# Routing of one batch and softmax of another in one timetable of joined runs, in an attention and mixture-of-experts kernel

## The chip, the cores and the metric

The kernel runs on one core of a Trainium2 chip, as a single launch. The time is the device time of one execution in microseconds (us); the median of several executions counts. TensorE (PE) does the matmuls and the transposes, with the weight loads (PEld) beside it; VectorE (DVE) and ScalarE (ACT) do the elementwise work; GpSimd (POOL) issues the indirect DMAs and SyncE (SP) the others.

## The reference

Three stages, all in float32. First a two-way attention without projections: 8 batches, 8 heads, 512 tokens `x` and 32 state rows per head, 64 wide. The tokens read the state (first softmax) and the state reads the tokens (second softmax). Then a feed-forward layer with hard-swish, 512 to 2048 to 512, over all 4608 rows. Then a mixture of 8 experts, one per row, with a second gate.

```python
scores = scale * np.matmul(x, state.transpose(0, 1, 3, 2))      # softmax -> a
xread = np.matmul(a, state)
scores2 = scale * np.matmul(state, x.transpose(0, 1, 3, 2))     # softmax -> a2
sread = np.matmul(a2, x)
...
h = x @ w_in
g = h * np.clip(h + 3.0, 0.0, 6.0) / 6.0
x = g @ w_out
...
logits = x @ w_gate
e_idx = np.argmax(logits, axis=1)
...
h = np.maximum(x[mask] @ w1[e], 0.0)
out[mask] = gate_w[mask, None] * eom[mask, e, None] * (h @ w2[e])
```

## The kernel before, in words

The work of the attention and the feed-forward layer is cut into segments, one per batch (`segs`, in the main loop at the end of what is printed below); batch 0 is cut in two halves of 8 f tiles, with batch 1 between them, and a last segment, of the rows that the states read, stands apart. An f tile is a slice of 128 of the 2048 hidden columns. For each f tile, `h_xread` makes six matmuls of 512 columns, `act` applies the hard-swish on ScalarE and VectorE (r at L419, g at L420, gh at L421, gl at L422), and `second` makes twelve matmuls in `gemm2` for the f tile two steps earlier, into four banks (o). These 18 matmuls of 512 columns are called the large ones here. `make_sw` multiplies the state into `w_in` once per four f tiles and batch: a run of eight small matmuls of shape 64\*32 (tile `misc`, operand `win`, L193), the state-weight run, whose result ScalarE (sh, L377) and VectorE (sl, L378) take out of two banks.

Into the segment of one batch are put two other pieces of work. The first is the routing of the batch before (`route`): the rows of its result are evicted (xr), turned by four transposes a tile of 128 rows (L460), copied (x2T, L461), multiplied with the two gates (the logits, L467, shape 128\*32), turned back (L473), and the expert is chosen by small steps of VectorE; two matmuls of 32 columns (L504, L505, the counts) give each row its place in its expert's list; then SP writes the rows (xd) and POOL scatters their token numbers into the table `tab` (L535). The second is the softmax of the next batch (`attn`): `attn_rows` begins with an x run (L193 with operand `xT`), scores of the state with the tokens, into two banks; VectorE transposes both (L273), finds the maxima of the second softmax (L317), ScalarE takes its exponentials (L321), and the first softmax follows in steps of 1024 elements (L287, L290, L291, L294, L299, L303, L307). `attn_cols` then turns the second softmax (L338), reads the tokens with it (L346, shape 128\*32, operand `xq`), and turns the result into x1 (L353), for heads e = 0 and 1 one after the other.

The bank `misc` has two buffers, which all small runs share; a list `users` holds who still reads the last ones. `halves`, used by the x run and the state-weight run, takes both buffers and makes its first matmul wait until both are free and all operands are there, so that the run isn't broken. All other small runs take one bank and are put where the framework's scheduler finds place. Both pieces of work are generators; the main loop takes one step of the routing from f tile 2 on and one of the softmax from f tile 3 on, one each per f tile (`step(later)`, `step(att)`). Each engine works its own queue in order.

Of the kernel before, what the change touches and what calls it, by code (L numbers as in the profile page):

```python
# [8 lines left out]
F32 = mybir.dt.float32  # L9
# [71 lines left out]
def tile_kernel(  # L81
# [60 lines left out]
    marks = []  # L142
# [13 lines left out]
    st_t, aT, loads, e2_t, x_in = {}, {}, {}, {}, {}  # L156

    def st_load(b):
        st_t[b] = ap.tile([128, 4, NS], F32, tag="st", name=f"st{b}")
        D.dma_start(st_t[b], sts[b])  # L160

    def x_loads(b):
        if b not in st_t:
            st_load(b)
        for k in range(2):
# [3 lines left out]
            loads[b, k] = x_t  # L169

    def q_loads(b):
        for k in range(2):
            x_q = ap.tile([128, 4, 256], F32, tag="x4", bufs=4, name=f"xq{b}_{k}")
            D.dma_start(x_q, xq[b, :, :, 256 * k:256 * k + 256])
# [7 lines left out]

    def halves(b, rhs, behind=()):

        behind = [*behind, *(i for u in users[-2:] for i in u)]
        made = [misc() for _ in range(2)]
        ps = [m[0] for m in made]
        first = None
        for j in range(4):
            for e in range(2):  # L190
                o = slice(64 * e, 64 * e + 64)
                r = rhs(j)[o]
                i = T.matmul(ps[e][32 * j:32 * j + 32, :r.shape[1]], st_t[b][o, j, :], r, start=True, stop=True,  # L193
                             tile_position=(64 * e, 32 * j))
                if first is not None:
                    tc.add_manual_dep(i.ins, first.name, LATER, reason="all at once")
                    continue
                first = i.ins
                for d in behind:
                    tc.add_manual_dep(first, d.name, DEP, reason="both banks are free and all of x is there")  # L200
        return ps, [m[1] for m in made]
# [109 lines left out]
    def columns(b, src, done=None):  # L311
# [3 lines left out]
        e2_t[b] = e2, s2, r2  # L315
        for e in range(2):
# [4 lines left out]
            j = S.activation(e2[e], src[e], AF.Exp, bias=nm[:, e:e + 1], scale=0.125, accum_out=s2[:, e:e + 1])  # L321
            if done:
                done[e] += [i.ins, j.ins]

    def attn_cols(b):
# [4 lines left out]
        e2, s2, r2 = e2_t.pop(b)  # L330
        x_q = [loads.pop((b, k, "q")) for k in range(2)]
        V.tensor_scalar(s2, s2, 1e-9, None, op0=ALU.add)
        V.reciprocal(r2, s2)
        read = ap.tile([128, 2, HD], F32, tag="wy", name="read", bufs=2)
        for e in range(2):
            psT, done = misc()
            for i in range(4):
# [816 lines left out]
```

## Time and profile before

| | us |
|---|---|
| median of 3 runs | 1150.56 |
| lowest and highest | 1149.32, 1151.2 |
| the profiled execution | 1145.18 |
| its span, first to last instruction | 1143.3 |
| TensorE busy | 1109.3 |
| VectorE busy | 697.5 |
| ScalarE busy | 559.9 |
| GpSimd busy | 137.0 |

The profile is of one execution. Busy time is the sum of an engine's instructions, with overlaps counted once. Matmuls are pipelined: each is shown with its full duration while the next one has begun, so that the distance of two starts is what a matmul costs. A run of equal instructions is one row with its count; a float32 matmul that TensorE makes in several passes is counted once a pass, so that a run of 16 read matmuls is shown as x32.

### The profile page before, as it was taken

What the parts mean: (1) busy time and instruction counts of PE and PEld (TensorE: products, weight loads), DVE (VectorE), ACT (ScalarE), POOL (GpSimd) and SP (SyncE); (2) the same over time, 40 slices, a digit from 0 to 9 for tenths busy, and PEclk for the clock granted to TensorE, in tenths of its full rate; (3) what the DMA queues carried; (4) which work ended last, traced back from release to release, by engine and by line L of the source; (5) the groups of instructions that cost most, each with busy time, mean ns of one, the idle gap of its engine ahead of it and who ended that gap; (6) DMA issues with size and microseconds to landing.
All of it is one profiled execution on the core that took longest, in us unless ns stands there. A gap on an engine that the chain in (4) does not pass through costs nothing.

```text
span 1143.3 us, 18670 instructions
## 1 busy us (share of the span) xinstructions
PE 1109.3 (97%) x7008; PEld 869.7 (76%) x7008; DVE 697.5 (61%) x1463; ACT 559.9 (49%) x1068; POOL 137.0 (12%) x172
## 2 busy tenths in 40 slices
PE   3899999999999999999999999999999999999997
PEld 1557776677677777777777788899969986999994
DVE  6997758744835736647445376876536644666661
ACT  3769734433333434433433345566546654666651
POOL 0000001010010100100101013242222212222101
PEclk9999999999999999999999999999999999999999
DMA  8834014210210211110101018386175768822400
GB/s 270 305 105 158 3 60 95 71 58 20 74 40 3 74 39 37 41 38 1 38 1 37 1 38 252 118 301 252 47 236 201 251 217 309 324 94 83 148 19 30
DMA packets 54463, 128.32 MB, mean 112 GB/s; under 512 B 6736, under 2 KB 25424, under 8 KB 54352
## 3 DMA queue, kind: packets, MB, share of 16 engines
q1 hardware_dynamic: 47072, 108.66, 28.7%
q0 software_dynamic: 7296, 18.41, 4.6%
q8 instruction: 57, 0.93, 0.4%
q14 instruction: 38, 0.31, 0.1%
HBM read 136.98 MB, written 19.57 MB: 137 GB/s over the span
## 4 chain that ended last, share of the span: by engine, by line
PE 89%; DVE 6%; ACT 1%; issue 1%; DMA 1%; SPq 0%; POOL 0%; POOLq 0%; ACTq 0%; DVEq 0%
PE h L797 16%; PE h L390 15%; PE o L429 10%; PE o L430 10%; PE o L428 10%; PE o L813 5%; PE o L817 5%; PE o L816 5%; PE misc L193 3%; PE h L404 2%; PE h L764 1%; PE misc L460 1%; PE misc L748 1%; PE o L783 1%; PE misc L346 1%
## 5 line engine op out<-in xcount | busy, mean ns | idle before, releaser
L429 PE MATMUL o<-wo,gh 128*128 128x512 f32 x512 | 203.6, 398 | 0.4 <-DVE wo L581 0.4
L428 PE MATMUL o<-wo,gh 128*128 128x512 f32 x512 | 199.8, 395 | 1.7 <-ACT wo L580 1.7
L430 PE MATMUL o<-wo,gl 128*128 128x512 f32 x512 | 200.5, 392 | 0.0
L420 DVE SCALAR_TENSOR_TENSOR g<-r,h 128x512 f32<-128x512 f32 x128 | 87.6, 684 | 116.1 <-ACT r L419 116.0
L803 DVE TENSOR_TENSOR vl<-w2s,vh 128x512 fp32r<-128x512 f32 x128 | 88.6, 692 | 106.2 <-ACT vh L802 87.3
L419 ACT ACTIVATE r<-h 128x512 f32<-128x512 f32 x128 | 76.5, 598 | 134.6 <-PE h L390 133.3
L802 ACT CAST vh<-w2s 128x512 fp32r<-128x512 f32 x128 | 79.4, 620 | 101.2 <-PE o L817 100.3
L422 DVE TENSOR_TENSOR gl<-g,gh 128x512 fp32r<-128x512 f32 x128 | 88.3, 690 | 53.7 <-ACT gh L421 53.0
L429 PEld LDWEIGHTS o<-wo,gh 128*128 128x128 f32 x512 | 96.2, 188 | 29.3 <-issue 9.4
L428 PEld LDWEIGHTS o<-wo,gh 128*128 128x128 f32 x512 | 95.8, 188 | 28.0 <-issue 4.4
L535 POOL DMA_INDIRECT tab<-toku,ldsti x34 | 34.4, 1011 | 658.9 <-DVE ldsti L530 593.8
L390 PE MATMUL h<-ah,sh 128*128 128x512 f32 x256 | 108.7, 426 | 4.5 <-ACT ah L256 3.0
L421 ACT CAST gh<-g 128x512 fp32r<-128x512 f32 x128 | 79.4, 620 | 68.1 <-DVE g L420 66.6
L430 PEld LDWEIGHTS o<-wo,gl 128*128 128x128 f32 x512 | 96.2, 188 | 20.2 <-issue 1.0
L793 DVE TENSOR_TENSOR wl<-w1s,wh 128x512 fp32r<-128x512 f32 x128 | 88.7, 693 | 30.0 <-ACT wh L792 23.3
L390 PE MATMUL h<-al,sh 128*128 128x512 f32 x256 | 102.9, 402 | 0.0
L390 PE MATMUL h<-ah,sl 128*128 128x512 f32 x256 | 100.8, 395 | 0.0
L817 PE MATMUL o<-vh,hl 128*128 128x512 f32 x256 | 100.3, 392 | 0.0
L816 PE MATMUL o<-vl,hh 128*128 128x512 f32 x256 | 100.1, 391 | 0.0
L792 ACT CAST wh<-w1s 128x512 fp32r<-128x512 f32 x128 | 79.5, 622 | 36.8 <-PE h L797 33.6
L797 PEld LDWEIGHTS h<-xh,wh 128*128 128x128 f32 x512 | 76.5, 188 | 11.7 <-issue 1.6
L797 PE MATMUL h<-xh,wh 128*128 128x256 f32 x512 | 82.8, 283 | 1.3 <-ACT xh L753 1.3
(223 smaller groups left out, 1829.8 us busy)
## 6 DMA issues: line engine op xcount, KB each, us to landing
w1s<-w SPq DMA_DIRECT2D x88, 512.0 KB
w2s<-w SPq DMA_DIRECT2D x88, 512.0 KB
xd<-xr SPq DMA_DIRECT2D x34, 256.5 KB
xT<-xT SPq DMA_DIRECT2D x16, 512.0 KB
wi<-w_in SPq DMA_DIRECT2D x16, 512.0 KB
wraw<-w_out SPq DMA_DIRECT2D x16, 512.0 KB
xq<-xq SPq DMA_DIRECT2D x16, 512.0 KB
half<-xp SPq DMA_DIRECT2D x4, 256.0 KB
```

The costliest lines, as they stand in the source:

```text
L390: T.matmul(ps, w[:, o:o + 128], a[:, e, :], start=(n == 0), stop=(n == 5))
L420: V.scalar_tensor_tensor(g6, r, 6.0, ps, op0=ALU.min, op1=ALU.mult)
L422: V.tensor_tensor(gl, g6, gh.bitcast(F32), op=ALU.subtract)
L428: T.matmul(po[t], gh[:, s], woh[ft], start=first, stop=False)
L429: T.matmul(po[t], gh[:, s], wol[ft], start=False, stop=False)
L430: T.matmul(po[t], gl[:, s], woh[ft], start=False, stop=last)
L792: S.copy(wh, a)
L793: V.tensor_tensor(wl, a, wh.bitcast(F32), op=ALU.subtract)
L797: T.matmul(ps, w[:, k, :], x[:, k, :], start=(m == 0), stop=(m == 11))
L803: V.tensor_tensor(vl, c, vh.bitcast(F32), op=ALU.subtract)
L816: T.matmul(py[t], hh[:, sl], vl, start=False, stop=False)
L817: T.matmul(py[t], hl[:, sl], vh, start=False, stop=(ft == 7))
```

## The change

The routing is cut into functions (`turn_rows`, `logits`, `turn_logits`, `choose`, `ranks`, `place`, `scatter`), and so is the second softmax (`cols_turn`, `cols_read`, `cols_x1`). `one_run` takes one or more such parts, allocates their banks, and issues all their matmuls behind each other; the first of them waits for the banks and the operands of all. In the segments of batches 2 to 6 a `timetable` says in which f tile each part is issued: at 2 and 3 the four transposed tiles of rows in two runs of eight; at 4 the x run; at 6 the turn of the columns for both e; at 7 the reads of both e and the logits of all four tiles as one run; at 8 x1 and the turn of the logits as one; the choice at 9, the counts at 10, rows and scatter at 11. In batch 7's segment there is no softmax, and the rest is done the same way. The second half of batch 0 has a table of its own. Batch 1's scatter moves from that half into batch 2's segment, behind the Relu of its fifth f tile, and that segment's x loads go behind an earlier Relu. The turned rows of tiles 2 and 3 take a buffer of the tag x4, which the loads of xT and xq share. No arithmetic is changed, and the matmuls are the same ones.

```diff
+    def x_loads(b, behind=()):
+        i = st_load(b)
+        for d in behind:
+            tc.add_manual_dep(i, d.name, DEP, reason="rows are written first")
...
+    def one_run(*parts):
+
+        behind = [i for u in users[-2:] for i in u]
+        built = [p() for p in parts]
+        first = None
+        for mms, needs, _ in built:
+            behind += needs
+        for mms, _, _ in built:
+            for m in mms:
+                i = m().ins
+                if first is not None:
+                    tc.add_manual_dep(i, first.name, LATER, reason="all at once")
+                    continue
+                first = i
+                for d in behind:
+                    tc.add_manual_dep(first, d.name, DEP, reason="banks are free and all operands are there")
+        for b in built:
+            b[2]()
+
+    def at_will(*parts):
+
+        for p in parts:
+            mms, _, use = p()
+            for m in mms:
+                m()
+            use()
...
+    def cols_turn(b):
+
+        e2, s2, r2, exps = e2_t.pop(b)
+        V.tensor_scalar(s2, s2, 1e-9, None, op0=ALU.add)
+        V.reciprocal(r2, s2)
+
+        def part():
...
+            return [lambda e=e, i=i: T.transpose(made[e][0][:, 128 * i:128 * i + 128],
+                                                 e2[e][:, 128 * i:128 * i + 128], ident)
+                    for e in range(2) for i in range(4)], exps, use
...
+            return [lambda e=e, i=i, j=j: mm(e, i, j) for e in range(2) for i in range(4) for j in range(4)], \
+                [*copies, *q_in[b]], use
...
-        read = ap.tile([128, 2, HD], F32, tag="wy", name="read", bufs=2)
-        for e in range(2):
-            psT, done = misc()
-            for i in range(4):
-                T.transpose(psT[:, 128 * i:128 * i + 128], e2[e][:, 128 * i:128 * i + 128], ident)
-            a2T = ap.tile([128, 4, 128], F32, tag="wy", name="a2T", bufs=2)
-            done.append(S.copy(a2T.rearrange("p a n -> p (a n)"), psT).ins)
-            yield
...
-            psR, done = misc()
-            for i in range(4):
-                for j in range(4):
-                    h = 2 * j + e
-                    T.matmul(psR[32 * j:32 * j + 32, :HD], a2T[:, i, 32 * j:32 * j + 32],
-                             x_q[h // 4][:, i, HD * (h % 4):HD * (h % 4) + HD], start=(i == 0), stop=(i == 3),
-                             tile_position=(0, 32 * j))
-            done.append(S.activation(read[:, e, :], psR[:, :HD], AF.Copy, scale=r2[:, e:e + 1]).ins)
-            yield
...
+        one_run(cols_turn(b))
+        yield
+        one_run(cols_read(b))
+        yield
+        one_run(cols_x1(b))
...
-        for t0 in range(0, nt, 2):
-            x2T = mp.tile([128, 4, 256], F32, tag="x2T", name="x2T", bufs=1)
-            for t in range(2):
-                ps, done = misc()
-                for k in range(4):
-                    T.transpose(ps[:, 128 * k:128 * k + 128], rows[t0 + t][:, 128 * k:128 * k + 128], ident)
-                done.append(V.tensor_copy(x2T[:, :, 128 * t:128 * t + 128],
-                                          ps.rearrange("p (k t) -> p k t", k=4)).ins)
-                if t == 0:
-                    yield
...
+            return [lambda t=t, k=k, ps=ps: T.transpose(ps[:, 128 * k:128 * k + 128],
+                                                        r.rows[t][:, 128 * k:128 * k + 128], ident)
+                    for t, (ps, _) in zip(ts, made) for k in range(4)], [r.made[t] for t in ts], use
...
+            return [lambda k=k, i=i: mm(k, i) for i in range(n // 2) for k in range(4)], list(r.copies), use
...
+    def scatter(r, behind=()):
 
         new = []
-        for t in range(nt):
-            i = G.indirect_dma_start(flat, bass.IndirectOffsetOnAxis(ap=dsti[:, t:t + 1], axis=0),
-                                     toku[:, tile0 + t:tile0 + t + 1], None).ins
+        for t in range(r.nt):
+            i = G.indirect_dma_start(flat, bass.IndirectOffsetOnAxis(ap=r.dsti[:, t:t + 1], axis=0),
+                                     toku[:, r.tile0 + t:r.tile0 + t + 1], None).ins
+            for d in behind:
+                tc.add_manual_dep(i, d.name, DEP, reason="rows are written first")
...
-        (1, 2): [I(10), go(cols[0], 2)],
-        (1, 3): [I(11), go(cols[0], 2)],
+        (1, 2): [I(10), go(cols[0])],
+        (1, 3): [I(11), go(cols[0])],
...
+    def timetable(b, r, att):
+
+        rows = attn_rows(b) if att else iter(())
+        todo = {}
+
+        def at(k, *fs):
+            todo.setdefault(k, []).extend(fs)
+
+        at(2, lambda: one_run(turn_rows(r, [0, 1])))
+        at(3, lambda: one_run(turn_rows(r, [2, 3], ap)))
+        for k in range(4, 10):
+            at(k, lambda: next(rows, None))
+        if att:
+            at(6, lambda: one_run(cols_turn(b)))
+            at(7, lambda: one_run(cols_read(b), logits(r, 0, 4)))
+            at(8, lambda: one_run(cols_x1(b), turn_logits(r, 0, 4)))
+        else:
+            at(6, lambda: one_run(logits(r, 0, 4)))
+            at(7, lambda: one_run(turn_logits(r, 0, 4)))
+        at(9, lambda: choose(r))
+        at(10, lambda: ranks(r))
+        at(11, lambda: place(r), lambda: scatter(r))
+        return todo
+
+    def half_timetable(b, r):
+
+        rows = attn_rows(b)
+        row = lambda: next(rows, None)
+        return {
+            2: [lambda: one_run(turn_rows(r, [0, 1]))],
+            3: [lambda: at_will(logits(r, 0, 2), turn_logits(r, 0, 2)), row],
+            4: [lambda: one_run(turn_rows(r, [2, 3])), row],
+            5: [lambda: at_will(logits(r, 2, 2), turn_logits(r, 2, 2)), lambda: choose(r), row],
+            6: [lambda: ranks(r), lambda: place(r), lambda: one_run(cols_turn(b)), row],
+            7: [lambda: one_run(cols_read(b)), row, row, lambda: one_run(cols_x1(b))],
+        }
...
-        att = [attn(nxt[0])] if n >= 2 and nxt[0] < NB else []
+        more = n >= 2 and nxt[0] < NB
+        late = n > 2
+        todo = {}
         for ft in range(f0, f1):
             h = h_xread(b, ft)
             with soon(b):
@@ -959,23 +1126,24 @@
             second(LAG)
             for x in plan.get((b, ft), []):
                 x()
-            if att and ft == f0 + 1:
-                x_loads(nxt[0])
-            if att and ft == f0 + 2:
+            if more and ft == f0 + 1 + late:
+                x_loads(nxt[0], marks[-2:-1] if n == 3 else ())
+            if n >= 2 and ft == f0 + 2:
+                r = later.pop()
+                todo = timetable(nxt[0], r, more) if late else half_timetable(nxt[0], r)
+                if n == 2:
+                    unplaced = r
+            if n == 3 and ft == f0 + 4:
+                scatter(unplaced, marks[-1:])
+            for x in todo.pop(ft - f0, []):
+                x()
+            if more and ft == f0 + 2 + late:
...
-            if ft - f0 >= 2:
-                step(later)
-            if ft - f0 >= 3:
-                step(att)
...
-        while att:
-            step(att)
-        while later:
-            step(later)
-        if nxt[0] < NB and n >= 2:
+        if more:
```

On TensorE, in batch 4's segment before, a logits run stands alone (its operand x2T holds two turned tiles of rows, l is its copied result), between large matmuls into h and o:

```order
L467 MATMUL misc<-x2T,wg_sb 32x256 x4
L390 MATMUL h<-al_3093,sh_1_1_3477 128x512
L390 MATMUL h<-ah_3092,sl_1_1_3478 128x512
L428 MATMUL o_3508<-wo_356,gh 128x512
L473 MATMUL misc<-ident,l_3573 128x128 x2
L429 MATMUL o_3508<-wo_356,gh 128x512
L430 MATMUL o_3508<-wo_356,gl 128x512
L428 MATMUL o_3509<-wo_356,gh 128x512
```

In the same segment after, the end of both reads (xq, with the turned second softmax a2T) and the logits of all four tiles:

```order
L386 MATMUL misc<-xq_0_3557,a2T 32x64 x2
L386 MATMUL misc<-xq_1_3559,a2T 32x64 x2
L553 MATMUL misc<-x2T,wg_sb 32x256 x8
L455 MATMUL h<-ah_3093,sh_2_0_3638 128x512
L455 MATMUL h<-al_3094,sh_2_0_3638 128x512
L455 MATMUL h<-ah_3093,sl_2_0_3639 128x512
```

The two logits runs and the two read runs have become one, ahead of a tile of h.

On VectorE, in batch 4's segment before, from the transposes behind the x run on (sm holds maxima and sums, bt the first softmax, x2T the turned rows):

```order
L273 STREAM_TRANSPOSE bt<-misc 128x512 x2
L317 TENSOR_REDUCE sm<-misc 128x1 x2
L320 TENSOR_SCALAR sm<-sm 128x1
L287 TENSOR_REDUCE sm<-bt 128x32
L320 TENSOR_SCALAR sm<-sm 128x1
L290 TENSOR_TENSOR bt<-bt,sm 128x1024
L461 COPY x2T<-misc 128x4x128
L420 SCALAR_TENSOR_TENSOR g_3644<-r,h 128x512
L294 TENSOR_REDUCE sm<-bt 128x32
L422 TENSOR_TENSOR gl<-g_3644,gh 128x512
L461 COPY x2T<-misc 128x4x128
```

The same place after:

```order
L301 STREAM_TRANSPOSE bt<-misc 128x512 x2
L345 TENSOR_REDUCE sm<-misc 128x1 x2
L348 TENSOR_SCALAR sm<-sm 128x1
L485 SCALAR_TENSOR_TENSOR g_3618<-r,h 128x512
L348 TENSOR_SCALAR sm<-sm 128x1
L315 TENSOR_REDUCE sm<-bt 128x32
L487 TENSOR_TENSOR gl<-g_3618,gh 128x512
L318 TENSOR_TENSOR bt<-bt,sm 128x1024
L357 TENSOR_SCALAR sm<-sm 128x2
L358 RECIPROCAL sm<-sm 128x2
L322 TENSOR_REDUCE sm<-bt 128x32
L443 TENSOR_TENSOR sl_2_0_3639<-misc,sh_2_0_3638 128x512
```

The copies of turned rows are gone from here, the whole chain of the first softmax up to its sum (L322) stands in one piece with one g and one gl in it, and right behind it come the subtractions sl of a state-weight run.

## Rows read from the trace of the kernel before

**Rows 1.** The page, busy us of an engine, share of the span and its instructions

```profile
PE 1109.3 (97%) x7008; PEld 869.7 (76%) x7008; DVE 697.5 (61%) x1463; ACT 559.9 (49%) x1068; POOL 137.0 (12%) x172
```

**Rows 2.** Stretch of one whole batch: busy us (instructions) by engine, granted clock, DMA

```profile
439.72:518.86 79.14, 78.88 (x481) 58.21 (x480) 44.96 (x95) 30.91 (x56) 3.82 (x4) 1.00 0.13 41
```

**Rows 3.** Timeline of TensorE, four transposes: start us, us, line, output<-operands, shape, count

```profile
518.86 0.60 PE L460 MATMUL misc<-ident,xr 128*128 128x128 f32 x4
519.21 0.48 PE L390 MATMUL h<-ah,sh 128*128 128x512 f32 x1
519.53 0.39 PE L390 MATMUL h<-al,sh 128*128 128x512 f32 x1
519.76 0.40 PE L390 MATMUL h<-ah,sl 128*128 128x512 f32 x1
```

**Rows 4.** The same view, eight transposes in one run

```profile
666.38 1.03 PE L460 MATMUL misc<-ident,xr 128*128 128x128 f32 x8
667.17 0.60 PE L404 MATMUL h<-x1h,wih 128*128 128x256 f32 x3
```

**Rows 5.** The same view, a logits run and the large matmuls around it

```profile
524.54 0.40 PE L390 MATMUL h<-ah,sh 128*128 128x512 f32 x1
524.87 0.64 PE L467 MATMUL misc<-x2T,wg_sb 128*32 128x256 f32 x8
525.44 0.50 PE L390 MATMUL h<-al,sh 128*128 128x512 f32 x1
525.77 0.39 PE L390 MATMUL h<-ah,sl 128*128 128x512 f32 x1
```

**Rows 6.** The same view, a read run of the second softmax

```profile
560.22 0.39 PE L430 MATMUL o<-wo,gl 128*128 128x512 f32 x1
560.53 0.65 PE L346 MATMUL misc<-xq,a2T 128*32 128x64 f32 x32
561.12 0.50 PE L390 MATMUL h<-ah,sh 128*128 128x512 f32 x1
561.46 0.40 PE L390 MATMUL h<-al,sh 128*128 128x512 f32 x1
```

**Rows 7.** The same view, the third transpose run of a batch

```profile
532.04 0.39 PE L430 MATMUL o<-wo,gl 128*128 128x512 f32 x1
532.44 0.33 PE L460 MATMUL misc<-ident,xr 128*128 128x128 f32 x1
```

**Rows 8.** The same view, the count matmuls, in brackets the idle time and what ended it

```profile
544.57 0.39 PE L428 MATMUL o<-wo,gh 128*128 128x512 f32 x1
545.22 0.18 PE L504 MATMUL misc<-loh,triu 128*128 128x32 bf16 x1 [0.26 <-DVE sl L378]
```

**Rows 9.** The same view, a state-weight run

```profile
276.19 1.09 PE L193 MATMUL misc<-win,st 64*32 64x512 f32 x16
277.21 0.50 PE L390 MATMUL h<-ah,sh 128*128 128x512 f32 x1
```

**Rows 10.** Timeline of ScalarE, the eviction of that run

```profile
277.37 1.07 ACT L377 CAST sh<-misc 128x512 fp32r<-128x512 f32 x2 [1.15 <-PE misc L193]
```

**Rows 11.** Timeline of VectorE behind an x run

```profile
291.56 1.31 DVE L273 STREAM_TRANSPOSE bt<-misc 128x512 f32<-128x512 f32 x2
292.79 1.25 DVE L317 TENSOR_REDUCE sm<-misc 128x1 f32<-128x512 f32 x2
297.00 0.68 DVE L420 SCALAR_TENSOR_TENSOR g<-r,h 128x512 f32<-128x512 f32 x1
297.61 1.22 DVE L294 TENSOR_REDUCE sm<-bt 128x32 f32<-128x1024 f32 x1
```

**Rows 12.** Timeline of ScalarE, exponential of the first softmax

```profile
296.52 1.06 ACT L291 ACTIVATE bt<-bt 128x1024 f32<-128x1024 f32 x1 [0.39 <-DVE bt L290]
```

**Rows 13.** Timeline of VectorE, the pair of sl subtractions

```profile
307.06 1.28 DVE L378 TENSOR_TENSOR sl<-misc,sh 128x512 fp32r<-128x512 f32 x2
```

**Rows 14.** Stretch in which two xq loads land, columns as in rows 2

```profile
254.00:260.00 6.00, 6.00 (x35) 4.89 (x28) 1.96 (x4) 1.53 (x3) 0.00 (x0) 1.00 0.54 175
```

More of the change, by code (lines that the diff above doesn't have):

```diff
@@ L169, in x_loads @@
             loads[b, k] = x_t
+            for d in behind:
+                tc.add_manual_dep(x_in[b, k], d.name, DEP, reason="rows are written first")
     def q_loads(b):
@@ L181, in misc, with mm @@
         return psum("misc", 2), users[-1]
-    def halves(b, rhs, behind=()):
[L185 to L188, printed above, removed]
-        for j in range(4):
-            for e in range(2):
+    def one_run(*parts):
[21 more added lines that the diff above has]
+            use()
+    def halves(b, rhs, behind=()):
+        got = []
+        def part():
+            got.extend(misc() for _ in range(2))
+            def mm(j, e):
                 o = slice(64 * e, 64 * e + 64)
                 r = rhs(j)[o]
[L193 to L201, printed above, removed]
+                return T.matmul(got[e][0][32 * j:32 * j + 32, :r.shape[1]], st_t[b][o, j, :], r, start=True, stop=True,
+                                tile_position=(64 * e, 32 * j))
+            return [lambda j=j, e=e: mm(j, e) for j in range(4) for e in range(2)], list(behind), lambda: None
+        one_run(part)
+        return [g[0] for g in got], [g[1] for g in got]
     def attn_rows_first(b):
@@ new lines, in cols_x1, with part, use @@
+    def cols_x1(b):
+        def part():
+            read, reads = e2_t.pop(b)
+            psX, done = misc()
+            psX = psX[:, :128]
+            def use():
+                hi, lo = [x[:, :, NS * b:NS * b + NS] for x in (x1h, x1l)]
+                src = psX.rearrange("p (j s) -> p j s", j=4)
+                done.append(V.tensor_copy(hi, src).ins)
+                done.append(V.tensor_tensor(lo, src, hi.bitcast(F32), op=ALU.subtract).ins)
+            return [lambda: T.transpose(psX, read, ident)], reads, use
+        return part
@@ new lines, in logits, with part, mm, use @@
+    def logits(r, t0, n):
+        def part():
+            psl, done = misc()
+            def mm(k, i):
+                return T.matmul(psl[32 * k:32 * k + 32, 256 * i:256 * i + 256], wg_sb[:, k, :],
+                                r.x2[t0 // 2 + i][:, k, :], start=True, stop=True, tile_position=(0, 32 * k))
+            def use():
+                r.l4 = mp.tile([128, 128 * n], F32, tag="x2T", name="l4", bufs=1)
+                done.append(S.copy(r.l4, psl[:, :128 * n]).ins)
+                r.l4_made = done[-1]
+            return [lambda k=k, i=i: mm(k, i) for i in range(n // 2) for k in range(4)], list(r.copies), use
+        return part
@@ L541, in route @@
         placed[:] = new
+    def route(r):
+        for t0 in range(0, r.nt, 2):
+            at_will(turn_rows(r, [t0]))
+            yield
+            at_will(turn_rows(r, [t0 + 1]), logits(r, t0, 2), turn_logits(r, t0, 2))
+            yield
+        choose(r)
+        ranks(r)
+        yield
+        place(r)
+        scatter(r)
         yield
```

197 lines of the change are left out of this document (113 added, 84 removed).

## The prediction

> **What bounds the kernel now.** I read the busy line of the page first, to find the engine that sets the span, then the table by stretches over one batch, then TensorE's timeline, matmul by matmul, around each small run, and last the other engines behind the run that the change moves closest to its successor. TensorE is busy 97% of the span [rows 1]. Over one whole batch segment it is busy 78.88 of 79.14 us at a granted clock of 1.00, VectorE 44.96 and ScalarE 30.91 [rows 2]. So in these segments nothing is won by making another engine faster. A microsecond is won only where TensorE's own queue gets shorter: there are no fewer matmuls, so it must be time lost around small runs, or a wait taken out. The large matmuls follow each other at 0.23 us (last two of [rows 3]); 288 of them make 65 of the 79 us, and the other 14 us are the small runs that the change rearranges.
>
> **Two kinds of small runs.** The transposes (128\*128 like the large matmuls) cost the same however they are grouped: four take 0.35 us to the next large matmul, whose successor comes at 0.32 instead of 0.23, 0.44 in all [rows 3]; eight in one run take 0.79 to the next matmul [rows 4], and with the same 0.09 that is 0.88, twice 0.44. Joining them saves nothing. The 128\*32 runs are different. The logits run begins 0.33 after the matmul ahead of it, and the matmul behind it is followed at 0.33, where 0.23 is usual: 0.10 at each end, 0.20 for a run, beside 0.57 of work [rows 5]. The read run, 0.59 of work, begins at 0.31 and is followed at 0.34 [rows 6], again 0.2. Joining two of these saves one such pair of ends.
>
> **The change part by part, in a full segment.** Five segments, those of batches 2 to 6, route the batch before and do the second softmax of the next by the new timetable; the work is the same, only in other groups. (a) Read, logits, logits and read stand alone before, in four runs, and are one run after: three pairs of ends, 3 x 0.20 = 0.60. What the seam between a read and a logits matmul costs no row shows, since they never touch before. Its bounds are nothing (the read run's 32 matmuls take 0.59 together, so they have no such gap among them [rows 6]) and 0.20 (as towards large matmuls [rows 5]); I take nothing, because both are of shape 128\*32. The Trainium skill (TensorEngine Tiling (Array Packing), Key Properties) says that TensorE drains when the tiling mode changes, and that going to another tile of a mode is no such change. By it the seam is free, as I take it; if the seams drained too, (a) would be nothing. (b) The third transpose run stands 17 large matmuls behind the x run and waits for its bank: it begins 0.40 after the matmul ahead of it where 0.23 is usual, 0.17 lost [rows 7]. After, the four are two runs ahead of the x run: 0.17 won. (c) The two count matmuls of the routing come 0.65 after the matmul ahead and sat idle 0.26 for an sl subtraction [rows 8]; after, they stand 18 large matmuls (4.1 us) behind the state-weight run whose bank they take, instead of 13, so I count 0.26. Together 1.03 us a segment.
>
> **What it may cost: the tight place.** In the order of after, a state-weight run comes 22 large matmuls behind the x run, and the turn of the columns 15 behind that. Each waits for two banks at once. I follow the chain from the x run's start. An 8-instruction run takes 1.02 to the next matmul, and an eviction behind it begins 1.18 after its start [rows 9, 10]. TensorE reaches the state-weight run at 1.02 + 0.11 + 22 x 0.227 + 0.10 = 6.2, and the turn at 6.2 + 1.13 + 15 x 0.227 = 10.75. VectorE, in the order of after: two transposes from 1.18 to 2.4, two maxima to 3.6 [rows 11], one small step, one g of 0.6 [rows 11] and another small step to about 4.4; on ScalarE a cast and the second exponential, 0.54 each by [rows 10], to about 5.6. That is before 6.2, no wait. Then, in steps as in [rows 11], the maximum of 1024 elements to 5.5, a gl to 6.1, the subtraction of 1.22 to 7.3; ScalarE's exponential of 1.06 to 8.4 [rows 12]; the sum, 1.2, to 9.55; and only then the pair of sl, 1.28 [rows 13], to 10.85. So the turn would wait some 0.1 to 0.2. I take 0.15; the bound from below is nothing, from above the 1.2 that one more step of 1024 elements adds. Behind the waiting turn are queued all of TensorE's matmuls. Net: 1.03 - 0.15 = 0.88 a segment, 4.4 for five. The other waits have room: the joined run needs the second half of xq, whose buffer is free only once the x run has read it, and two such loads of 0.5 MB lie within 6 us [rows 14], where 14 us pass from the x run to the joined run. The writes of the rows and the scatter come some four f tiles later than before, on SP's and POOL's queues, ahead of nothing that this stage waits for.
>
> **The other segments.** Batch 1's segment joins two pairs of read runs: 2 x 0.20 = 0.4. The last batch's segment joins two logits runs, 0.20, and its count matmuls stand further back as in (c), say another 0.2: 0.4. The half segment of batch 0, eight f tiles long, joins its reads and is rid of one wait as in (b), 0.4 together; but there the joined read stands only 4 large matmuls (0.9 us) behind the turn, and ScalarE must copy two banks, 1.07 [rows 10], after the 0.16 until it can start: a wait of 0.3, and the chain to the counts is as packed as before. I take nothing, with 0.7 to either side. Batch 1's scatter goes behind a Relu of the next segment on POOL, and the x loads of that segment behind another Relu on SP; the loads behind those are needed 10 us later. Nothing. From the last batch's counts on, every engine's order is the one of before, so the last 480 us move as a block.
>
> **The sum.** 4.4 + 0.4 + 0.4 + 0 = 5.2 us. The profiled execution's own time is 1145.18, with a span of 1143.3; after, 1140.0 and 1138.1. The median of the runs is 1150.56, 5.4 above the profiled one; 5.2 less is 1145.4.
>
> **The rivals.** First, seams cost what ends cost: (a) and the joined reads and logits elsewhere give nothing, and a segment wins 0.17 + 0.26 - 0.15 = 0.28. That is 1.4, with 0.2 in the last batch 1.6: 1149.0, within what counts as the same. For it speaks that no row shows the two kinds in one run; against it, that the matmuls inside a run show no gap. Second, slower: VectorE comes late to the chain, and the turn of the columns becomes the place where TensorE waits. The two copies of the turned rows, a g and a gl, 0.6 each, stand right ahead of the transposes in VectorE's order. If these four still have to be done when the x run ends, the chain is 2.4 longer, and each microsecond is paid five times. Without any wait the five segments win 5.15 and the others 0.8; the kernel wins nothing from a wait of 1.2 us a segment on, and is slower by 0.2% (2.3 us, about what a measurement can tell from no change) from 1.65 on. At 0.15 + 2.4 it loses 5 x 2.55 - 5.95 = 6.8: 1157.4. For it speaks that the chain has no slack by my count; against it, that those rows are turned 18 large matmuls, 4.1 us, ahead of the x run, and the four steps take 2.4. Third, (a) holds, but the waits of (b) and (c) come back in other places, a bank freed late at the x run or at the counts: 5 x (0.60 - 0.15) + 0.8 = 3.05, 1147.5.
>
> **How the numbers follow.** The forecast, 1145.4, has 0.55; its own range is 1142 (no wait at the turn, the half segment winning 0.7, the joined run's inner work shorter) to 1147. The third rival, 0.2, is a smaller gain of the same sign. The first, 0.15, is no difference, and the slower one has 0.1. Faster by over 0.2% (below 1148.26): 0.55 + 0.2, and a little of the first, 0.77; within: 0.14; slower: 0.09. The range for 8 in 10 reaches from 1141.5 to 1150, so that it takes in the first and third rivals and leaves out the slower one.
>
> **What the profile after would show.** Right: reads and logits as one 128\*32 run with 0.10 lost ahead and behind, some 2.5 us in all; each full segment at about 78.3 us; no idle ahead of the counts; the turn of the columns 0 to 0.3 us late. Wrong: a gap between the reads and the logits (first rival), TensorE idle on sl ahead of the turn by over a microsecond (second), or idle ahead of the x run or of the counts (third). What would make all of it wrong is a loss outside these segments, above all in the last 480 us, where I expect the same times.

## The result, and the profile after

The changed kernel took **1137.43 us**, the median of six runs (1135.85 to 1139.82), against 1150.09 for the kernel before (six runs, 1147.56 to 1151.2): a ratio of 0.9893, 95% interval 0.9882 to 0.9904, or 12.7 us. The forecast was 1145.4 with a range from 1141.5 to 1150. The sign was right; the gain was more than twice the forecast, and outside the range.

The two traces alone give less: 1139.82 us (span 1138.0) against 1145.18 (span 1143.3), 5.4 us. Two things hide in that. The start differs by chance from run to run: the first evictions of batch 0's first half began at 76.58 us before and at 78.38 after, though all that stands ahead of them is the same. And, as the experiments below show, the profiled run of the kernel before had been spared a stall that its timed runs probably had. On which chip it ran is not on record.

To leave the start out, I cut both traces where batches end, at their first evictions. Windows of the kernel before, with columns for length, busy time (instructions) of PE, PEld, DVE, ACT and POOL, granted clock, DMA share, GB/s:

```profile
76.58:151.48 74.90, 74.90 (x492) 57.03 (x491) 54.50 (x98) 58.39 (x109) 0.00 (x0) 1.00 0.31 101
151.48:274.25 122.77, 122.50 (x783) 88.97 (x782) 77.23 (x170) 48.49 (x90) 7.81 (x8) 1.00 0.26 62
274.25:353.43 79.18, 78.92 (x480) 58.21 (x479) 44.96 (x94) 30.92 (x57) 3.83 (x4) 1.00 0.14 41
...
590.81:664.53 73.72, 73.54 (x387) 57.12 (x386) 35.86 (x78) 26.55 (x48) 4.57 (x4) 1.00 0.05 15
664.53:712.64 48.11, 48.11 (x318) 42.43 (x317) 33.42 (x110) 23.13 (x52) 12.66 (x21) 1.00 0.53 157
```

The same windows of the kernel after:

```profile
78.38:152.55 74.17, 74.17 (x492) 57.20 (x491) 54.26 (x98) 57.57 (x109) 0.00 (x0) 1.00 0.33 103
152.55:275.28 122.73, 120.61 (x783) 89.71 (x782) 78.11 (x169) 47.95 (x90) 8.08 (x8) 1.00 0.26 58
275.28:352.83 77.55, 77.55 (x480) 58.61 (x479) 45.96 (x93) 30.55 (x56) 3.82 (x4) 1.00 0.17 42
...
585.44:658.53 73.09, 73.09 (x387) 57.36 (x386) 36.17 (x77) 26.34 (x47) 3.83 (x4) 1.00 0.06 15
658.53:706.67 48.14, 48.14 (x316) 42.25 (x315) 33.59 (x110) 23.07 (x52) 12.26 (x21) 1.00 0.52 141
```

| stretch (its end: first evictions of ...) | before | after | gain | forecast |
|---|---|---|---|---|
| batch 1's segment | 74.90 | 74.17 | 0.73 | 0.4 |
| second half of batch 0 and batch 2's segment | 122.77 | 122.73 | 0.04 | 0 + 0.88 |
| segments of batches 3 to 6 | 4 x 79.1 | 4 x 77.55 | 6.4 | 4 x 0.88 |
| batch 7's segment | 73.72 | 73.09 | 0.63 | 0.4 |
| last segment | 48.11 | 48.14 | 0 | 0 |

In all 7.8 us from the traces, where 5.2 were forecast: a full segment wins 1.56 to 1.63 instead of 0.88, and the second row loses what batch 2's segment wins. TensorE, idle 0.26 us in a segment before [rows 2], is busy for all of the 77.55. Where a segment's 1.6 us come from is read on TensorE's timeline (start, length, line, output<-operands, shape, count):

```profile
458.24 0.39 PE L455 MATMUL h<-ah,sh 128*128 128x512 f32 x1
458.51 1.09 PE L371 MATMUL misc<-ident,e 128*128 128x128 f32 x8
459.36 0.48 PE L455 MATMUL h<-al,sh 128*128 128x512 f32 x1
459.68 0.40 PE L455 MATMUL h<-ah,sl 128*128 128x512 f32 x1
...
463.12 0.39 PE L495 MATMUL o<-wo,gl 128*128 128x512 f32 x1
463.44 1.10 PE L386 MATMUL misc<-xq,a2T 128*32 128x64 f32 x64
464.35 1.05 PE L553 MATMUL misc<-x2T,wg_sb 128*32 128x256 f32 x16
465.33 0.50 PE L455 MATMUL h<-ah,sh 128*128 128x512 f32 x1
465.67 0.40 PE L455 MATMUL h<-al,sh 128*128 128x512 f32 x1
...
479.38 0.39 PE L495 MATMUL o<-wo,gl 128*128 128x512 f32 x1
479.61 0.19 PE L613 MATMUL misc<-loh,triu 128*128 128x32 bf16 x1
479.65 0.18 PE L614 MATMUL misc<-loh,ones 128*128 128x32 bf16 x1
479.68 0.48 PE L455 MATMUL h<-ah,sh 128*128 128x512 f32 x1
480.00 0.40 PE L455 MATMUL h<-al,sh 128*128 128x512 f32 x1
```

Measured from the start of the large matmul ahead of a run to the start of the second one behind it, less two usual steps of 0.227, a run's cost is what it adds to TensorE's queue. The joined read and logits run costs 465.67 - 463.12 - 0.45 = 2.10. Before, a read run cost 561.46 - 560.22 - 0.45 = 0.79 [rows 6] and a logits run 525.77 - 524.54 - 0.45 = 0.78 [rows 5], the four 3.11 by the means of three segments: **1.01 saved**, 0.60 forecast. The counts cost 0.17 where they cost 0.56 [rows 8]: 0.40 saved, 0.26 forecast. The transposed rows cost 2 x 0.89 instead of 2.02 together: 0.24, forecast 0.17. The turn of the columns (0.99) lost 0.09 against 2 x 0.45, forecast 0.15, and x1 with the turned logits won 0.04. Sum 1.60.

The loss in the second row of the table is one place. VectorE and TensorE in the second half of batch 0 (in brackets the idle time ahead and what ended it):

```profile
193.10 0.40 PE L495 MATMUL o<-wo,gl 128*128 128x512 f32 x1
193.87 0.69 DVE L516 SCALAR_TENSOR_TENSOR xr<-o,part 128x512 f32<-128x512 f32 x1 [1.00 <-DMA xd<-xr]
194.47 0.28 DVE L412 TENSOR_TENSOR x1l<-misc,x1h 128x128 fp32r<-128x128 f32 x1
...
194.90 1.09 PE L223 MATMUL misc<-win,st 64*32 64x512 f32 x16 [1.41 <-DVE x1l L412]
...
196.71 0.50 PE L455 MATMUL h<-ah,sh 128*128 128x512 f32 x1 [0.71 <-ACT sh L442]
197.04 0.39 PE L455 MATMUL h<-al,sh 128*128 128x512 f32 x1
```

An eviction of batch 0 (L516) waits until the write of batch 1's row, out of the row buffer that it needs, has ended. x1's low part (L412), ready since x1's high part at 192.59, is queued behind it on VectorE; behind that the state-weight run waits, and behind that run TensorE's whole queue: 1.41 + 0.71 us. By the distance of the large matmuls this state-weight run costs 197.04 - 193.10 - 0.45 = 3.49, where the usual one costs 1.22: 2.3 lost. The half segment's own runs win 0.6 (its reads cost 1.24 instead of 1.60, its transposed rows 1.81 instead of 2.02), and batch 2's segment its 1.6.

### The profile page after: what moved, and what is told of

The parts are those of the page before. It is cut to its first block, busy times and chain, and to the rows that moved or that the text cites. A ratio compares the mean times of both kernels' runs of the same rounds, so it can differ in the third digit from the quotient of the medians.

```text
span 1138.0 us, 18621 instructions
## 1 busy us (share of the span) xinstructions
PE 1102.1 (97%) x7008; PEld 873.1 (77%) x7008; DVE 703.2 (62%) x1457; ACT 556.6 (49%) x1062; POOL 134.7 (12%) x172
## 4 chain that ended last, share of the span: by engine, by line
PE 90%; DMA 4%; DVE 2%; issue 1%; ACT 1%; SPq 0%; POOL 0%; POOLq 0%; ACTq 0%; DVEq 0%
PE h L455 16%; PE h L925 16%; PE o L493 10%; PE o L495 10%; PE o L494 10%; PE o L941 5%; PE o L945 5%; PE o L944 5%; PE misc L223 4%; PE h L892 1%; PE misc L541 1%; PE misc L876 1%; PE o L911 1%; DMA w2s<-w 1%; DMA wi<-w_in 1%
```

## The experiments

The traces explain 7.8 us of 12.7. So there were two questions: are the prices above the right ones, and where are the other 5 us? Each row of the table is one chip, with runs of the kernel before beside the other kernels. "Trunk" is the trace's time from the first evictions of batch 0's first half to those of the last segment: 636.1 us in the traces of the kernel before but one, 627.4 to 628.3 in the four of the changed kernel.

| chip | kernel before | other kernels |
|---|---|---|
| first | 1150.09 | changed 1137.43 |
| second | 1145.69 | b_again 1146.09, b_scatter_later 1146.66, a_scatter_at_once 1142.72, a_logits_apart 1138.69 |
| third | 1149.55 | a_again 1137.06, a_x1_first 1135.06, a_half_early 1134.82, a_early_at_once 1134.89 |
| fourth | 1145.37 | b_third 1144.99, b_scatter_third 1145.67 |
| fifth | 1149.23 | a_third 1136.59, b_fourth 1150.28, b_scatter_fourth 1145.80 |
| sixth | 1149.17 | a_fourth 1138.01, a_half_early_2 1135.17 |

The kernel before takes some 1145.5 us on two chips and 1149 to 1150 on the others.

**The price of a run: a_logits_apart.** The changed kernel with the joined runs taken apart.

```diff
-            at(7, lambda: one_run(cols_read(b), logits(r, 0, 4)))
-            at(8, lambda: one_run(cols_x1(b), turn_logits(r, 0, 4)))
+            at(7, lambda: one_run(cols_read(b)))
+            at(8, lambda: one_run(cols_x1(b)))
+            at(9, lambda: one_run(logits(r, 0, 4)))
+            at(10, lambda: one_run(turn_logits(r, 0, 4)))
```

> The changed kernel with the reads, x1, the logits and the turn of the logits as four runs of their own in f tiles 7 to 10, in the five full segments; the choice, the counts and the places two f tiles later. Seams free at 0.20 us a lost pair of ends: two joins a segment undone, 5 x 0.40 = 2.0 us, 1139.4. The trace of the changed kernel shows the joined run at 2.10 and L386 x64 alone at 1.24, L553 x16 alone in batch 7's segment at 1.21: 0.35 for this join, with some 0.2 for x1 and the turned logits 0.55 a segment, 2.7 us, 1140.2. Rival (a seam costs what an end costs, and the gain came from other things): 1137.4, within 0.5.

A segment takes 77.89 instead of 77.55, 0.34 more, 1.7 for five; the trunk is 629.9, 1.6 to 2.5 over the changed kernel's. Its timeline:

```profile
461.25 0.39 PE L495 MATMUL o<-wo,gl 128*128 128x512 f32 x1
461.57 1.10 PE L386 MATMUL misc<-xq,a2T 128*32 128x64 f32 x64
462.60 0.50 PE L455 MATMUL h<-ah,sh 128*128 128x512 f32 x1
462.93 0.40 PE L455 MATMUL h<-al,sh 128*128 128x512 f32 x1
...
470.81 0.39 PE L495 MATMUL o<-wo,gl 128*128 128x512 f32 x1
471.13 1.07 PE L553 MATMUL misc<-x2T,wg_sb 128*32 128x256 f32 x16
...
472.47 0.40 PE L455 MATMUL h<-al,sh 128*128 128x512 f32 x1
```

All reads in one run cost 1.23, all logits 1.21. The timed 1138.69 lies below both forecasts, and the changed kernel did not run on this chip, so that it is the trace that decides. Each of the three joins brings the same: reads 2 x 0.79 - 1.23 = 0.35, logits 2 x 0.78 - 1.21 = 0.35, the two together 1.23 + 1.21 - 2.10 = 0.34. So a 128\*32 run among 128\*128 matmuls costs 0.34 us here beside its inner work, with reads or with logits in it, and the seam is free within 0.01. Joining x1 with the turned logits, all 128\*128, brings nothing (0.13 + 0.45 apart, 0.57 joined): my second 0.20 in that expectation was wrong.

**The other 5 us: a second trace, and the deferral alone.** b_again is the kernel before unchanged. b_scatter_later is the kernel before with one part of the change only:

```diff
-                x_loads(nxt[0])
+                x_loads(nxt[0], marks[-1:] if n == 3 else ())
+            if n == 3 and ft == f0 + 4:
+                unplaced.pop()(marks[-1:])
```

> The kernel before, unchanged, for a second profile. Its median was 1150.1 us and its one profiled run 1145.18, 4.9 below; the changed kernel's profiled run was 1139.82, 2.4 above its median of 1137.43. So the two traces differ by 5.3 us and the medians by 12.7. Theory A (a transfer stalls the usual run of the kernel before, and the profiled one was lucky): a second profile of 1149 to 1152 us shows a wait of about 5 us that the first does not have, most likely at 185 to 205 us, where rows, token numbers and loads of the next batch go out together. Theory B (chance in the start, the first 85 us): the second profile has the same stretch lengths from 86 us on within 1 us, and differs ahead of it.

> The kernel before with one part of the change alone: batch 1's token numbers are scattered behind the Relu of f tile 4 of batch 2's segment, and that segment's x loads go behind the Relu ahead. Theory A (the missing 5 us are contention of these transfers): 1144.5 to 1146 us against 1150.1. Theory B (all of the gain is in TensorE's order): 1149.5 to 1150.7, the same as before. My forecast had nothing for this part.

On this chip both took what the kernel before takes, 1145.69 (ratios 1.0000, interval 0.9991 to 1.0009, and 1.0006, interval 0.9997 to 1.0015); the trunk was 636.1 in both. So far Theory A had fallen. But the kernel before was 4.4 us lower here than in the first comparison, and that was the missing amount.

**The deferral undone in the changed kernel: a_scatter_at_once.**

```diff
-                x_loads(nxt[0], marks[-2:-1] if n == 3 else ())
+                x_loads(nxt[0])
-            if n == 3 and ft == f0 + 4:
-                scatter(unplaced, marks[-1:])
```

with `scatter(r)` right behind `place(r)` in the half segment.

> The changed kernel with batch 1's scatter right behind its places, and the x loads of batch 2's segment not behind a Relu: the deferral undone. Theory A: 1141.5 to 1143 us against 1137.4. Theory B: 1136.9 to 1138.1.

On the same chip, where the deferral is worth nothing to the kernel before, undoing it costs the new order 4.5 us by the traces: a trunk of 632.6, and 1142.72, 4.0 over a_logits_apart, itself slower than the changed kernel. VectorE, TensorE, a window just behind, and the second stretch of the table above:

```profile
197.15 0.69 DVE L516 SCALAR_TENSOR_TENSOR xr<-o,part 128x512 f32<-128x512 f32 x1 [4.49 <-DMA xd<-xr]
197.75 1.28 DVE L443 TENSOR_TENSOR sl<-misc,sh 128x512 fp32r<-128x512 f32 x2
...
198.49 0.50 PE L455 MATMUL h<-ah,sl 128*128 128x512 f32 x1 [2.66 <-DVE sl L443]
...
200.00:202.00 2.00, 2.00 (x14) 0.60 (x18) 0.83 (x2) 1.09 (x3) 0.00 (x0) 0.50 0.78 133
150.47:277.70 127.23, 122.67 (x783) 90.00 (x782) 78.34 (x169) 48.14 (x89) 7.80 (x8) 0.99 0.26 56
```

With the scatter and the x loads issued at once, a row's write takes so long to end that the fourth eviction waits 4.49 us; which of the two holds it up is not separated. sl stands behind it, TensorE idles 2.66, and right after that the granted clock is 0.50, the lower of its two levels, so that part of the idle time is paid once more in slow matmuls: against the changed kernel's stretch, 122.73 with 120.61 busy, 2.4 us more are idle and 2.1 more are busy.

**The half segment: a_x1_first, a_half_early, a_early_at_once.** The first puts the four evictions behind x1's low part on VectorE:

```diff
+            if part is not None:
+                tc.add_manual_dep(i.ins, x1_made[2].name, LATER, reason="x1 is first")
```

The second begins the softmax of batch 2 one f tile earlier, so that only one eviction is left ahead of sl; the third is the second without the deferral:

```diff
-            2: [lambda: one_run(turn_rows(r, [0, 1]))],
+            2: [lambda: one_run(turn_rows(r, [0, 1])), row],
...
-            6: [lambda: ranks(r), lambda: place(r), lambda: one_run(cols_turn(b)), row],
-            7: [lambda: one_run(cols_read(b)), row, row, lambda: one_run(cols_x1(b))],
+            6: [lambda: choose(r), lambda: one_run(cols_read(b)), row, row],
+            7: [lambda: ranks(r), lambda: place(r), lambda: one_run(cols_x1(b))],
```

> The changed kernel, unchanged, for a second profile and beside the kernel before on one chip. From the end of the first half of batch 0 to the end of the program its first trace is 7.9 us shorter than both traces of the kernel before; what lies ahead of that moves by chance (the first evictions began between 75.6 and 78.4 us in six traces). Theory of the trace: 7.5 to 8.5 us below the kernel before, 0.7 to 0.75%. If instead the first comparison's 12.7 us (1.1%) come again, there is something that no trace shows yet, and this profile would have to show where.

> The changed kernel with the four evictions of batch 0's second half put behind x1's low part (L412) in VectorE's order. In the changed kernel the third of them waits 1.00 us for a row buffer whose write is still under way, x1's low part stands behind it, and the state-weight run behind that idles 1.41 us at 194.90. Theory (head of the queue): this idle goes, 1.2 to 1.6 us less than the unchanged one. Rival (the chain of x1 is that long by itself, or the four evictions now hold up sl): within 0.4 of it.

> The changed kernel with the softmax of batch 2 one f tile earlier in the second half of batch 0: the x run in f tile 2 of it, the turn of the columns in 5, the reads in 6, the choice in 6; batch 1's counts and places at 7 with x1. In the order sl of batch 2's first state-weight run then stands behind one eviction instead of four, and three large matmuls stand behind the run. The two idle stretches of 1.41 (x1's low part) and 0.71 (sh) go or shrink: 1.4 to 2.3 us less than the changed kernel. Rival (VectorE is late elsewhere in the half segment, the counts or the turn of the columns wait): 0 to 2 us more.

> The same as the one before, with batch 1's scatter and batch 2's x loads not deferred. In the changed kernel undoing the deferral cost 4.5 us of trace time (the fourth eviction waited 4.49 us for a row's write, and sl behind it). Theory (the scatter costs only by way of the evictions that wait for row buffers ahead of sl): with one eviction ahead of sl the loss is 0 to 1.5 us. Rival (the transfers hold TensorE up by themselves, through loads that come late): 3.5 to 5 us again.

The trunks are 628.1, 626.5, 625.7 and 625.7: 1.6 us by the order of one VectorE instruction against four, 2.4 by the earlier softmax. In the timed runs 2.0 and 2.2. In a_half_early TensorE has no wait left there, and the window that was 122.73 is 120.38, all of it busy:

```profile
190.41 0.29 DVE L412 TENSOR_TENSOR x1l<-misc,x1h 128x128 fp32r<-128x128 f32 x1
192.69 0.69 DVE L516 SCALAR_TENSOR_TENSOR xr<-o,part 128x512 f32<-128x512 f32 x1 [1.99 <-PE o L495]
193.29 1.28 DVE L443 TENSOR_TENSOR sl<-misc,sh 128x512 fp32r<-128x512 f32 x2
...
152.65:273.03 120.38, 120.38 (x783) 89.74 (x782) 78.72 (x169) 48.14 (x90) 8.09 (x8) 1.00 0.24 59
```

And a_early_at_once, with the scatter and the x loads at once, loses nothing (1134.89; trunk 625.7). So in the new order, as far as this chip and the second show, these transfers cost time only through the evictions that wait for row buffers ahead of sl. a_again repeats the first comparison's ratio (0.9887, interval 0.9866 to 0.9909), and not the 7.5 to 8.5 us that the traces had made me expect.

**A trace of the stall: b_third and b_scatter_third, then a_third, b_fourth and b_scatter_fourth.** Unchanged kernels and the deferral alone, on further chips.

> The kernel before, unchanged, for a profile on a chip where it takes about 1150 us (it took 1145.7 on the chip of its second profile and 1149.6 on the chip where the changed kernel was 12.5 us faster; all its traces so far are of the lower kind). Theory A (contention of the row writes, the scatter and the loads in the second half of batch 0, which on such a chip reaches TensorE): a profile of 1148 to 1152 us is 3 to 6 us longer between the evictions of batch 1 and those of batch 2 (122.8 us in the traces so far), with TensorE idle at about 195 us behind an eviction or sl, and no other stretch is longer by over 0.5 us. Theory B (the chip's start or its last stage is longer): this stretch stays within 0.5 us of 122.8.

> The kernel before with the deferral of batch 1's scatter and batch 2's x loads alone, on the same chip as the run ahead of it. Theory A: where the kernel before takes about 1150 us, this takes 1144.5 to 1146.5, so that the deferral alone is worth 4 to 5 us there; where the kernel before takes 1145.7, no difference, as in the first comparison of the two. Theory B: the same as the kernel before on either chip, within 1 us.

> The changed kernel, unchanged, on one more chip. The kernel before takes 1145.4 to 1145.7 us on two chips and 1149.6 to 1150.1 on others; the traces of both kernels give a difference of 8.0 us (636.1 against 628.1 between the first and the last evictions). Theory C (the kernel before, and not the changed one, has something that costs 4.5 us more on some chips): where the kernel before takes 1145.5 this takes 1137 to 1138, 0.7% less; where it takes 1150, again 1137, 1.1% less. Rival (the changed kernel is lower on some chips as well): where the kernel before takes 1145.5 this takes 1133, 1.1% less there too.

> The kernel before, unchanged, for a trace on a chip where it takes about 1150 us. If it takes 1150 here, its trace shows where the 4.5 us lie: Theory A, between the evictions of batch 1 and those of batch 2 (122.8 us in three traces of the other kind); Theory B, ahead of the first evictions (75.6 to 78.5 us) or behind the last (418.2 to 418.7). If it takes 1145.5 again, nothing follows from it.

> The kernel before with the deferral alone. Where the kernel before takes 1150: Theory A 1144.5 to 1146.5; Theory B 1149 to 1151. Where it takes 1145.5: the same as it, as on two chips.

The fourth chip was of the kind where the kernel before takes 1145.4, and nothing followed. The fifth was of the other kind, and b_fourth's profiled run took 1150.44 (span 1148.5). Its windows:

```profile
77.02:151.92 74.90, 74.90 (x492) 57.03 (x491) 54.49 (x98) 58.38 (x110) 0.00 (x0) 1.00 0.32 101
151.92:279.29 127.37, 124.39 (x783) 89.46 (x782) 77.23 (x170) 48.51 (x91) 7.82 (x8) 0.99 0.29 60
279.29:358.42 79.13, 78.86 (x480) 58.21 (x479) 44.97 (x94) 30.91 (x57) 3.83 (x4) 1.00 0.15 41
191.00:192.00 1.00, 0.00 (x0) 0.00 (x0) 0.00 (x0) 0.00 (x0) 0.69 (x2) 1.00 0.97 171
192.00:193.00 1.00, 0.00 (x0) 0.00 (x0) 0.00 (x0) 0.02 (x1) 0.69 (x2) 1.00 0.32 1
194.00:195.00 1.00, 1.00 (x4) 0.61 (x2) 0.34 (x2) 0.00 (x0) 0.00 (x0) 0.50 0.82 25
```

All stretches are those of the other traces but one: 127.37 instead of 122.77, **4.6 us**, the missing amount: 2.7 more idle, and 1.9 more busy (124.39 instead of 122.50). In it, on TensorE and ScalarE, and last SyncE's waits for the x loads (us in all, times, longest):

```profile
190.26 0.39 PE L430 MATMUL o<-wo,gl 128*128 128x512 f32 x1
193.34 0.37 PE L353 MATMUL misc<-ident,read 128*128 128x128 f32 x1 [2.69 <-issue]
...
192.98 0.31 ACT L349 ACTIVATE read<-misc,sm 128x64 f32<-128x64 f32 x1 [3.84 <-remote]
SPq L168 <- remote: 3.2, 2, 2.9
```

The same in the first trace of the kernel before, with the wait of the first of the two loads:

```profile
189.64 0.31 ACT L349 ACTIVATE read<-misc,sm 128x64 f32<-128x64 f32 x1 [0.94 <-PE misc L346]
190.05 0.29 PE L353 MATMUL misc<-ident,read 128*128 128x128 f32 x1
SPq L168 <- PE misc L346: 0.6, 1, 0.6
```

From 190.7 to 193 us TensorE, ScalarE and VectorE all stand still. They stand in one chain: TensorE's next run, L353, turns what ScalarE's L349 takes out, in both traces 0.1 us or less behind it, and VectorE's next step needs L353. So what is late is L349. It begins 3.65 us after the first of its read matmuls (189.33), where it is 0.75 without the stall (188.89), and SyncE's first x load, which without the stall is released by the same matmuls, is late by 2.2 us too. Batch 1's rows and its scatters are on the DMA engines then: their share is 0.97 at 171 GB/s from 191 to 192, but 0.32 at 1 GB/s from 192 to 193, when L349 still waits. The x loads are issued only at 192.24, so that of the two things deferred they cannot have begun the stop. From 193.5 to nearly 197 TensorE runs at a granted clock of 0.50. On the same chip b_scatter_fourth, the deferral alone, took 1145.80 (ratio to the kernel before 0.9969, interval 0.9959 to 0.9979), with this stretch back at its usual length:

```profile
152.19:275.01 122.82, 122.58 (x783) 88.96 (x782) 77.25 (x170) 48.54 (x90) 8.21 (x8) 1.00 0.25 62
```

So Theory A holds on this kind of chip: the deferral alone is worth 3.4 to 4.5 us to the kernel before there, and nothing on the others. The trunk agrees: 640.6 in b_fourth and 627.4 in a_third, 13.2, beside 12.6 in their runs' medians (1149.23, 1136.59). The changed kernel itself was never run beside a kernel before of 1145.5; a_logits_apart was, and was 7.0 lower where its trunk is 6.2 shorter.

**The better version again: a_fourth and a_half_early_2.**

> The changed kernel, unchanged, beside the version with the earlier softmax in the half segment. It took 1136.6 to 1137.4 us in three comparisons; 1136 to 1138 again, 0.7% below the kernel before where that takes 1145.5 and 1.1% below where it takes 1150.

> The version with the softmax of batch 2 one f tile earlier in the half segment, once more, to see its gain in timed runs: its trace is 2.4 us shorter than the changed kernel's between the first and the last evictions. Theory: 1.5 to 3 us below the changed kernel on the same chip, 1134 to 1135.5. Rival (given back by chance in the start): within 0.7 us of it.

1138.01 and 1135.17, ratios 0.9901 (0.9885 to 0.9918) and 0.9872 (0.9855 to 0.9888). The intervals just touch; with the first pair (0.9887 and 0.9864) and trunks 1.7 and 2.4 us apart, the earlier softmax in the half segment is some 2.2 to 2.8 us below the changed kernel, 14 below the kernel before.

## Why the prediction was wrong, step by step

- **What bounds the kernel: right.** All gains are places where TensorE's queue got shorter or a wait went; no other engine became the bound, and from the last segment on nothing changed (48.11 and 48.14; the rest, 430.66 and 431.33, lies between 430.6 and 431.4 in all traces).
- **(a), the join of reads and logits: right mechanism, mis-sized term.** Forecast 3 x 0.20 = 0.60, measured 1.01. The step that failed is "0.10 at each end, 0.20 for a run, beside 0.57 of work": I took as lost only the gaps that rows show at the ends, and as work all that lies between. The work itself was not 0.57: doubling it in one run added 0.43 to 0.44, so 0.14 of what I called work was paid once a run as well. The bound of the forecast's own range ("the joined run's inner work shorter") names it, but gives it no number. The seam was free, as I took it: 2.10 is one 0.34 and the inner work of both, 0.87 and 0.88, within 0.01. The Trainium skill (TensorEngine Tiling (Array Packing), Key Properties) has TensorE drain when the tiling mode changes, not when the tile alone does; 0.34 for a run and nothing at the seam agree with it. The first rival, seams that cost what ends cost, is refuted.
- **(b) and (c): right mechanism, too small.** 0.24 for 0.17 and 0.40 for 0.26. For (c) I used the idle time in brackets, which begins at the modelled end of the matmul ahead; the distance of starts, 0.65 where 0.23 is usual [rows 8], held 0.42. For (b) I counted only the late start; by that distance the third transpose run costs 0.67 where the others cost 0.45.
- **The tight place: right.** 0.09 where I took 0.15. The slower rival did not come near.
- **The half segment: wrong.** I took nothing, 0.7 to either side, and named a wait of 0.3 for ScalarE's copies. That wait did not come: the joined reads cost 1.24 there, and 1.23 where nothing could hold them up. Batch 2's segment wins its 1.6 by the trace, and the two together 0.04: the half segment lost about 1.5 (0.8 to 1.6 over the four traces of the changed kernel, whose stretch takes 121.94 to 122.79). I had followed TensorE and ScalarE there and never asked what stands ahead of x1's low part on VectorE; in the order it is a batch 0 eviction that needs a row buffer, and the writes of these rows are issued 3.0 us ahead of the first of these evictions (187.19 and 190.17), where it was 4.0 (187.05 and 191.07), and that eviction has itself waited for one of them. a_x1_first shows this place alone to be worth 1.6.
- **The deferral of the scatter: wrong.** "The loads behind those are needed 10 us later. Nothing." I asked who needs the moved transfers, and not whom they disturb where they stood. It took away a stall of 4.6 us on the fifth chip, and probably on the three others where the kernel before takes as long, the first comparison's among them; no trace there shows it. And on the second chip the new order would have lost 4.5 without it.
- **The sum: wrong in its last line.** "5.4 above the profiled one; 5.2 less is 1145.4" carried the distance of the profiled run from the median over as a constant. It was no constant: a profiled run 4 us below the lowest of three timed ones [1145.18 against 1149.32] was a run without some stall that the others had, and the change took away just that stall. Whether it was spared by chance or ran on a chip of the other kind is not on record.

By size: of 12.7 us, 5.2 were forecast; 4.1 more came from mis-sized terms (0.7 in each of five full segments, 0.3 in batch 1's, 0.2 in batch 7's), 4.6 from the stall, if the first chip is like the fifth, and 1.5 were lost in the half segment. That makes 12.4.

What stays open: why L349 and the x load are released 2 to 3 us late in b_fourth. The profile names no releaser ("remote"), and since it models the ends of matmuls, it does not tell whether the read matmuls themselves ended late or only the signal of their end came late. With the x loads not yet issued, the scatter beside the row writes is left of what the deferral moves; how it does this no run shows. Nor do the runs show what differs between the chips.

## What to carry to other kernels

Price a small run on a full TensorE by the distance between the starts of the large matmuls around it, not by the gaps that rows show; in this kernel a join of two 128\*32 runs is then worth 0.34 us, and a join of two 128\*128 runs nothing. When the profiled run is below every timed run, look for a stall that this trace doesn't hold, and treat each part of the change that moves transfers as one that may remove it. When several engines stop at once, look which of them merely wait for another: here three stood still for one late release. Of a step that is squeezed into a shorter segment, read every engine's queue at the place, VectorE's above all: an eviction that waits for a buffer still being written holds up whatever is queued behind it.

## What the runs showed of the hardware

The same program differed by 4 us between chips, in one stretch of a trace. On the fifth, with row writes and small scatters in flight, ScalarE and SyncE were released 2.9 and 2.2 us late behind the same read matmuls, and TensorE stood idle for 2.7 us; in a trace without the stall the rows were issued at the same time, 110.47 us after the first evictions in both. And a stop of 2.7 us costs more than itself: behind it the granted clock was 0.50 for some 3 us, 1.2 GHz instead of 2.4, in the kernel before (193.5 to nearly 197 us in b_fourth) as in the changed one (200 to 203 us in a_scatter_at_once). The shorter stops of 1.41 and 0.71 us in the changed kernel were not followed by it (granted clock 1.00 over that stretch).
